# A reciprocal sent through DRAM in place of TensorE broadcasts, and a third Strassen chunk, in a four-layer linear-attention kernel

## The chip, the cores and the metric

The kernel runs on one core of one Trainium2 chip. The metric is device time of that core in microseconds (us), the median of several runs. A run that took over 1.5% longer than the fastest of the same kernel counts as slow and is left out.

## The reference

Two attention layers and two feed-forward layers (FFN) alternate on 2048 tokens of width 512. The attention is linear: no softmax, but a positive feature map, and every query's result is divided by a denominator per head.

```python
def _A_ref(x, wqkv, wo):                       # 32 heads of 16
    qkv = (x @ wqkv)...                        # (cut) split in q, k, v by head
    phi = lambda t: jnp.where(t > 0, t + 1, jnp.exp(t)) + 1e-6
    pq, pk = phi(q), phi(k)
    kv  = jnp.einsum("bhsd,bhse->bhde", pk, v)
    z   = jnp.einsum("bhsd->bhd", pk)
    num = jnp.einsum("bhqd,bhde->bhqe", pq, kv)
    den = jnp.einsum("bhqd,bhd->bhq", pq, z)[..., None] + 1e-6
    return (num / den)... @ wo                 # (cut) heads put back in a row

def _B_ref(x, w1, w2):                         # 512 -> 1376 -> 512
    return jnp.maximum(x @ w1, 0) @ w2

x = A_x
x = x + _A_ref(_layernorm(x), A_wqkv, A_wo)
x = x + _B_ref(_layernorm(x), B_w1, B_w2)
x = x + _A_ref(_layernorm(x), A_wqkv, A_wo)
x = x + _B_ref(_layernorm(x), B_w1, B_w2)
```

## The kernel before

The kernel works in four chunks of 512 tokens per layer. Python code lists all operations once (`g.add` with an engine, what is read, what is written and an estimated duration), and two tables of numbers, `ORDER` and `BANKS`, fix the order in which every engine gets them, the engine of each operation that may run on two (a letter after its number: a for ScalarE, d for VectorE), and the PSUM bank of each result.

The denominators of a chunk come out of four small matmuls that run side by side, each on its own 32 output rows. ScalarE takes a logarithm and an exponential of the negative, which is 1/den for 32 heads. That has to be spread over the 16 features of each head before it can multiply the query features:

```python
def a_den_inv(t, b):
    us = [pq_unit(j, t) for j in range(4)]
    mm_group(lambda: [(psv[32*j:32*j+32, b, :], Zc[:, j, :], unit_ap(us[j]), True, True, False) for j in range(4)], ...)
    ...
    g.add(ACT, lambda e: e.activation(lden[:, s, :], psv[:, b, :], ACTF.Ln, bias=eps6[:, 0:1]), ...)
    g.add(ACT, lambda e: e.activation(lden[:, s, :], lden[:, s, :], ACTF.Exp, scale=-1.0), ...)
    g.add(DVE, lambda e: e.tensor_copy(rhi[:, s, :], lden[:, s, :]), ...)             # bf16 high part
    g.add(DVE, lambda e: e.scalar_tensor_tensor(rsp[:, s, :], rhi[:, s, :], rneg[:, 0:1], lden[:, s, :],
                                                ALU.mult, ALU.add), ...)              # high rows and low rows
    return s

def a_den_mul(t, s, GB):
    us = [pq_unit(j, t) for j in range(4)]
    mm_group(lambda: [(psv[:, GB[j], :], esel[32*j:32*j+32, :], rsp[32*j:32*j+32, s, :], True, True, False)
                      for j in range(4)], ...)                                        # broadcast to 128 rows
    for j in range(4):
        g.add(DVE, lambda e, j=j: e.tensor_tensor(unit_ap(us[j]), unit_ap(us[j]), psv[:, GB[j], :], ALU.mult), ...)
```

In an FFN a chunk's first matmul is done either plainly (`b_h`) or in one level of Strassen (`b_h_str`): seven half-size products in place of eight, for the price of sums of token blocks and of weight blocks on VectorE and of copies between PSUM banks. A parameter names the Strassen chunks of each FFN:

```python
HSTR=[(2, 3), (1, 2, 3)]          # first FFN: chunks 2 and 3; second FFN: chunks 1, 2 and 3
...
hs = HSTR[layer // 2]
for t in range(NCH):
    steps.append((t, None, lambda t=t: b_h_str(t, layer) if t in hs else b_h(t)))
    if t >= 1:
        steps.append((None, None if last_layer else t - 1, lambda t=t: o_step(t - 1)))
```

## Time and profile before

| Kernel before | |
|---|---|
| device time, median of 4 runs | 275.53 us (275.16 to 275.73) |
| span of the profiled run, granted clock | 273.7 us, 0.999 |
| TensorE busy | 267.7 us, 98% |
| VectorE busy | 242.0 us, 88% |
| ScalarE busy | 198.8 us, 73% |
| moved by DMA | 18.35 MB in 41976 packets |

The span is what the profile sees between the first and the last instruction; the device time is some 1.7 us longer. "Busy" adds up the intervals in which an engine had an instruction in flight. It does not say whether an instruction that took longer was waiting for something inside, and of TensorE it says little, because matmuls overlap (one of 512 columns is shown as busy for 379 ns, and the next starts after 216). So the working below takes the distance between starts of consecutive matmuls as their cost. The page, the waits, the stretches and the groups of this kernel are shown in the prediction.

### The profile page before, as it was taken

What the parts mean: (1) busy time and instruction counts of PE and PEld (TensorE: products, weight loads), DVE (VectorE), ACT (ScalarE), POOL (GpSimd) and SP (SyncE); (2) the same over time, 40 slices, a digit from 0 to 9 for tenths busy, and PEclk for the clock granted to TensorE, in tenths of its full rate; (3) what the DMA queues carried; (4) which work ended last, traced back from release to release, by engine and by line L of the source; (5) the groups of instructions that cost most, each with busy time, mean ns of one, the idle gap of its engine ahead of it and who ended that gap; (6) DMA issues with size and microseconds to landing.
All of it is one profiled execution on the core that took longest, in us unless ns stands there. A gap on an engine that the chain in (4) does not pass through costs nothing.

```text
span 273.7 us, 5259 instructions
## 1 busy us (share of the span) xinstructions
PE 267.7 (98%) x1956; PEld 168.0 (61%) x1975; DVE 242.0 (88%) x633; ACT 198.8 (73%) x429; POOL 19.3 (7%) x30
## 2 busy tenths in 40 slices
PE   8999999999999999999999999999999999999995
PEld 3444454444467488888864445355448787888863
DVE  5999799999998998899999837999999899999864
ACT  3988757999974795876679969489998735875320
POOL 3111000000102101000111000000010020110000
PEclk9999999999999999999999999999999999999999
DMA  6955940030462093001226100003310322411012
GB/s 201 383 110 114 294 161 0 13 66 1 77 58 40 6 130 59 4 0 22 39 40 126 27 0 5 0 2 77 60 19 0 79 40 64 111 23 77 2 77 77
DMA packets 41976, 18.35 MB, mean 67 GB/s; under 512 B 36352, under 2 KB 40544, under 8 KB 41952
## 3 DMA queue, kind: packets, MB, share of 16 engines
q1 hardware_dynamic: 41808, 17.96, 28.0%
q8 instruction: 15, 0.25, 0.4%
q14 instruction: 9, 0.07, 0.1%
q10 hardware_dynamic: 144, 0.07, 0.1%
HBM read 7.01 MB, written 2.10 MB: 33 GB/s over the span
## 4 chain that ended last, share of the span: by engine, by line
PE 89%; DVE 5%; ACT 3%; issue 1%
PE ps L535 87%; DVE big L849 2%; PE ps L419 2%; ACT escr L517 2%; ACT big L515 1%; DVE big L521 1%; DVE xn L575 1%; DVE escr L519 0%; ACT big L1016 0%; DVE xn L965 0%; PE ps L498 0%; DVE rsp L839 0%; ACT xn L472 0%; DVE KVT L650 0%; ACT xn L553 0%
## 5 line engine op out<-in xcount | busy, mean ns | idle before, releaser
L517 ACT ACTIVATE escr<-ps 128x512 bf16<-128x512 f32 x60 | 35.4, 611 | 5.8 <-PE ps L535 4.9
L515 ACT ACTIVATE big<-ps 128x512 bf16<-128x512 f32 x60 | 35.5, 612 | 4.3 <-PE ps L535 4.2
L542 ACT ACTIVATE sqscr<-xres 128x512 bf16<-128x512 f32 x48 | 30.1, 627 | 7.3 <-DVE xres L579 3.9
L535 PE MATMUL ps<-big,xn 128*128 128x512 bf16 x123 | 30.2, 379 | 0.3
L535 PE MATMUL ps<-gw,big 128*128 128x512 bf16 x120 | 29.7, 379 | 0.4
L535 PE MATMUL ps<-wqkv,Tb 128*128 128x512 bf16 x124 | 29.7, 379 | 0.4 <-DVE Tb L506 0.2
L1016 ACT ACTIVATE big<-ps 128x512 bf16<-128x512 f32 (+1 forms) x42 | 21.9, 530 | 9.7 <-PE ps L535 9.2
L535 PE MATMUL ps<-Tb,w 128*128 128x512 bf16 x120 | 28.7, 379 | 0.0
L535 PE MATMUL ps<-Tb,wqkv 128*128 128x512 bf16 x112 | 26.6, 379 | 0.0
L521 DVE TENSOR_TENSOR big<-big,escr 128x512 bf16<-128x512 bf16 x60 | 24.2, 421 | 2.4 <-ACT big L515 1.5
L535 PE MATMUL ps<-w,xin 128*128 128x256 bf16 (+1 forms) x190 | 26.1, 272 | 0.0
L519 DVE TENSOR_SCALAR escr<-escr 128x512 bf16<-128x512 bf16 x60 | 16.5, 287 | 7.3 <-ACT escr L517 6.9
L535 PE MATMUL ps<-w2s,big 128*128 128x256 f16 x160 | 21.7, 272 | 0.0
L535 PEld LDWEIGHTS ps<-wqkv,Tb 128*128 128x128 bf16 x128 | 12.3, 98 | 14.7 <-ACT Tb L505 0.7
L535 PEld LDWEIGHTS ps<-big,xn 128*128 128x128 bf16 x128 | 12.0, 98 | 14.6 <-issue 0.9
L849 DVE TENSOR_TENSOR big<-big,ps 128x512 bf16<-128x512 bf16 x32 | 20.5, 680 | 0.5 <-PE ps L535 0.3
L535 PE MATMUL ps<-w,big 128*128 128x256 f16 (+2 forms) x113 | 20.6, 302 | 0.0
L535 PEld LDWEIGHTS ps<-w,xin 128*128 128x128 f16 x190 | 18.3, 98 | 3.7 <-ACT hrt L871 0.2
L568 POOL TENSOR_TENSOR rstdf<-varf,nhalf 128x4 f32<-128x4 f32 x8 | 8.8, 1109 | 161.5 <-DVE varf L566 137.3
L535 PEld LDWEIGHTS ps<-gw,big 128*128 128x128 bf16 x128 | 12.0, 98 | 13.1 <-issue 0.5
L535 PEld LDWEIGHTS ps<-Tb,w 128*128 128x128 bf16 x120 | 11.4, 98 | 12.7 <-issue 0.5
L1099 ACT ACTIVATE ps<-ps 128x256 f32<-128x256 f32 x22 | 8.1, 369 | 15.2 <-PE ps L535 15.0
(154 smaller groups left out, 523.2 us busy)
## 6 DMA issues: line engine op xcount, KB each, us to landing
wqkv<-in_A_wqkv_dram SPq DMA_DIRECT2D x3, 512.0 KB, 7.3
xin<-in_A_x_dram SPq DMA_DIRECT2D x3, 512.0 KB, 8.1
out_dram<-xn SPq DMA_DIRECT2D x3, 512.0 KB, 2.7
w<-in_B_w_dram SPq DMA_DIRECT2D x1, 1376.0 KB, 6.7
w<-in_B_w_dram SPq DMA_DIRECT2D x1, 1280.0 KB, 9.9
wo<-in_A_wo_dram SPq DMA_DIRECT2D x1, 512.0 KB, 10.3
Tb<-xn SPq DMA_TRANSPOSE x30, 3.2
xin<-in_A_x_dram SPq DMA_DIRECT2D x1, 384.0 KB, 3.1
```

Of the source, the lines that this page charges most:

```text
L419: last = e.matmul(psv[:, wt, :], wrm[:, 0:128], wrm[:, :], start=True, stop=True)
L515: g.add(ACT, lambda e: e.activation(dst_ap, psv[:, b, :], ACTF.Identity, bias=1.0 + 1e-6, scale=1.0), [("ps", b)], [dst_key], C_ACT_PSUM, ...
L517: g.add(ACT, lambda e: e.activation(escr[:, s, :], psv[:, b, :], ACTF.Exp), [("ps", b)], [("escr", s)], C_ACT_EXP, name=name + "_exp")
L519: g.add(DVE, lambda e: e.tensor_scalar(escr[:, s, :], escr[:, s, :], 1.0, 1e-6, ALU.min, ALU.add), [("escr", s)], [("escr", s)], C_DVE_BF4 ...
L521: g.add(DVE, lambda e: e.tensor_tensor(dst_ap, dst_ap, escr[:, s, :], ALU.max), [dst_key, ("escr", s)], [dst_key], 340.0, name=name + "_phi")
L535: last = e.matmul(o, l, r, start=st, stop=sp, skip_group_check=skip)
L542: g.add(ACT, lambda e: e.activation(sqscr[:, q, :], xres[:, i, :], ACTF.Square, accum_out=dst[:, i:i + 1]), [("xres", i)], [("sqscr", q), ...
L568: g.add(POOL, lambda e: e.tensor_tensor(rstdf[:, sl], varf[:, sl], nhalf[:, 0:4], ALU.pow), [("varf", t), ("nhalf",)], [("rstdf", t)], C_P ...
L575: g.add(DVE, lambda e: e.scalar_tensor_tensor(xn[:, i, :], psv[:, b, :], rstdf[:, i:i + 1], xres[:, i, :], ALU.mult, ALU.add), rd, [("xn", ...
L849: g.add(DVE, lambda e, j=j: e.tensor_tensor(unit_ap(us[j]), unit_ap(us[j]), psv[:, GB[j], :], ALU.mult), [("big", us[j]), ("ps", GB[j])], ...
L1016: g.add_flex([(ACT, lambda e: e.activation(out_ap(r, m), pv(b), ACTF.Relu), cost(C_ACT_PSUM)), (DVE, lambda e: e.tensor_scalar(out_ap(r, m ...
L1099: g.add_flex([(ACT, lambda e: e.activation(psv[:, c1, cols], psv[:, c2, L], ACTF.Identity), 290.0), (DVE, lambda e: e.tensor_copy(psv[:, c ...
```

## The change

There are two parts, and a new order.

**Part 1.** 1/den is written by the exponential as bf16 straight into `rsp`, stored to DRAM, and read back four times, each read taking 8 rows (8 heads) and repeating each of them 16 times, so that 128 partitions are filled. No TensorE broadcast is left, and no split into high and low parts; the multiplication reads SBUF instead of PSUM. The query projections of the last two chunks of the first attention come late (`QL`).

**Part 2.** The first FFN also gets three Strassen chunks. The weight sums `WN` are kept in one place for both FFNs.

```diff
-HSTR=[(2, 3), (1, 2, 3)]
+HSTR=[(1, 2, 3), (1, 2, 3)]
-QL=(3,)
+QL=(2,)
+        rdram = nc.dram_tensor("rdram", [2, NCH, 128, 512], BF16, kind="Internal").ap()
...
-            g.add(ACT, lambda e: e.activation(lden[:, s, :], lden[:, s, :], ACTF.Exp, scale=-1.0), ...)
-            g.add(DVE, lambda e: e.tensor_copy(rhi[:, s, :], lden[:, s, :]), ...)
-            g.add(DVE, lambda e: e.scalar_tensor_tensor(rsp[:, s, :], rhi[:, s, :], rneg[:, 0:1], lden[:, s, :], ALU.mult, ALU.add), ...)
+            g.add(ACT, lambda e: e.activation(rsp[:, s, :], lden[:, s, :], ACTF.Exp, scale=-1.0), ...)
+            r = rdram[cur_layer[0] // 2, t]
+            dma(lambda e: e.dma_start(r, rsp[:, s, :]), [("rsp", s)], [("rd", t)], 400.0, "rw%d" % t)
+            for j in range(4):
+                i = 4 * t + j
+                dma(lambda e, i=i, j=j: e.dma_start(xn[:, i, :], r[32 * j:32 * j + 8, :].unsqueeze(1).broadcast_to([8, 16, 512])),
+                    [("rd", t)], [("xn", i)], 650.0, "rb%d_%d" % (t, j))
...
-            mm_group(lambda: [(psv[:, GB[j], :], esel[32 * j:32 * j + 32, :], rsp[32 * j:32 * j + 32, s, :], True, True, False)
-                              for j in range(4)], ...)
             for j in range(4):
-                g.add(DVE, lambda e, j=j: e.tensor_tensor(unit_ap(us[j]), unit_ap(us[j]), psv[:, GB[j], :], ALU.mult), ...)
+                i = 4 * t + j
+                g.add(DVE, lambda e, j=j, i=i: e.tensor_tensor(unit_ap(us[j]), unit_ap(us[j]), xn[:, i, :], ALU.mult), ...)
...
-        WN = {1: [... slots(gw_f, "gw", range(3))], 3: [... slots(xin_f, "xin", range(3))]}
+        WN = [(a, [k] + own) for a, k, own in slots(xin_f, "xin", range(3))]
...
-                out[n] = (ap, key)
+                out[n] = (ap, [key] + own)
... (cut: ORDER and BANKS, all numbers new; the places of the row sums, and what else follows from the moved buffers; EARLY, the places of eight sums
     of the second attention; the place of one step of the FFN; the constants for the low parts, which are gone)
```

The last hunk makes the row sums of the second FFN matmul name the buffers under them as well as their own key when they are read. Without it, an order that moves the next writer of such a buffer forward has a race.

## The prediction

> **What bounds the kernel now.** I read the page's busy table first, then its slices, the chain of work that ended last, the waits of TensorE, the stretches of both attention stages, and at last the timeline around the instructions that the change touches.
>
> ```profile
> PE 267.7 (98%) x1956; PEld 168.0 (61%) x1975; DVE 242.0 (88%) x633; ACT 198.8 (73%) x429; POOL 19.3 (7%) x30
> PE   8999999999999999999999999999999999999995
> DVE  5999799999998998899999837999999899999864
> PEclk9999999999999999999999999999999999999999
> PE 89%; DVE 5%; ACT 3%; issue 1%
> ```
>
> The reader sees TensorE busy in every slice at full clock, and 89% of the last chain on it. A busy matmul row need not be a full one, so I looked for idle time and for spacing. The waits of TensorE matmuls hold two entries:
>
> ```profile
> PE ps L419 <- DVE wrm L412: 1.2, 1, 1.2
> PE ps L535 <- DVE Tb L506: 0.2, 1, 0.2
> ```
>
> Both are in the first 9 us. I then took start to start times of consecutive matmuls from the trace: the medians are 216 ns for 512 columns, 109 ns for 256 and 43 ns for 96. After the head (up to 8.6 us) nearly every pair stands at its median. About seventeen gaps are longer by 216 ns almost exactly, which is one 512-column matmul whose record is missing, not idle time. Real slack is about 0.1 us near 180 us and 0.6 us between 262 and 266 us. So what bounds the kernel is **the number of columns TensorE streams**, plus a head of 8.6 us and 3.5 us after the last matmul starts. A change shortens it only by taking TensorE time away, and lengthens it only by opening gaps.
>
> The second engine is close behind, which the stretches show (columns: us, then busy us of PE, PEld, DVE, ACT, POOL with counts):
>
> ```profile
> 38.00:58.00 20.00, 19.87 (x119) 8.77 (x118) 19.19 (x47) 16.16 (x31) 0.00 (x0) 1.00 0.14 27
> 58.00:74.00 16.00, 15.84 (x97) 7.11 (x96) 15.86 (x46) 15.38 (x36) 1.01 (x1) 1.00 0.13 25
> 74.00:110.00 36.00, 35.89 (x277) 25.31 (x278) 32.46 (x88) 25.52 (x58) 4.00 (x4) 1.00 0.43 60
> ```
>
> VectorE is at 96% and 99% in the first attention's end, 90% in the FFN after it.
>
> **What the Trainium skill says, and whether the trace agrees.** (1) "TensorE: Matmul & The Clock Gate", section "Wait — 56ns, not 53.3ns?", gives a warm spacing of N/2.4 GHz plus about 2.5 ns, 215.7 ns for 512 columns; this trace has 216. (2) "TensorEngine Tiling (Array Packing)", section "Key Properties": "Mode switching requires drain". The trace agrees: before each tiled group the spacing is 93 to 96 ns over the median. (3) "VectorE: DVE Perf Modes", section "What auto-detection actually checks": a two-source operation runs two elements per cycle only if every tensor is 16-bit with step one. The trace agrees: 421 ns with bf16 operands alone, 680 ns with the fp32 PSUM operand. (4) "DMA: Bandwidth & Descriptors", section "Anatomy of one DMA — SWDGE (gpsimd) path", fits a fixed cost of about 2.0 us for the GpSimd-issued path. Here the SyncE queue issues; its 128 KB transfers take 1.7 us (store) and 2.4 us (load), so the same order, and I use the trace's figures.
>
> **Part 1, the reciprocal.** For each of 8 chunks (4 in each attention layer) the kernel before turns the denominators into bf16 high and low rows, broadcasts them with four 32-row matmuls, and multiplies from PSUM. This is the timeline of TensorE at one chunk, then the groups concerned:
>
> ```profile
> 170.64 1.24 PE L535 MATMUL ps<-big,xn 128*128 128x512 bf16 x5
> 171.81 0.40 PE L535 MATMUL ps<-rsp,esel 32*128 32x512 bf16 x4
> 172.14 1.04 PE L535 MATMUL ps<-big,xn 128*128 128x512 bf16 x4
> L849 DVE TENSOR_TENSOR big<-big,ps 128x512 bf16<-128x512 bf16 x32 | 20.5, 680 | 0.5 <-PE ps L535 0.3
> L521 DVE TENSOR_TENSOR big<-big,escr 128x512 bf16<-128x512 bf16 x60 | 24.2, 421 | 2.4 <-ACT big L515 1.5
> L839 DVE SCALAR_TENSOR_TENSOR rsp<-rhi,rneg,lden 128x512 bf16<-128x512 bf16 x8 | 6.0, 751 | 0.2
> L838 DVE CAST rhi<-lden 128x512 bf16<-128x512 f32 x8 | 3.4, 421 | 0.2 <-ACT lden L836 0.2
> ```
>
> TensorE, removed: the four matmuls run side by side. The next matmul starts 172.14 - 171.81 = 0.33 us later, and the drain ahead costs 0.095 us: 0.423 us a group. Six groups stand alone, 6 x 0.423 = 2.54 us. Two stand just ahead of the denominator matmuls, which are tiled too and will then pay the drain themselves: one saves 0.33 us, the other, which had a wait of 0.1 us in it, 0.45 us. Sum **3.3 us**, all on the path, since TensorE has no slack.
>
> VectorE, removed: the cast (0.42) and the subtraction (0.75) go. Four multiplications cost 0.62 each back to back now (2.48 us for four in the timeline) and should cost 0.375 each with bf16 operands in SBUF (0.76 us for two of the L521 kind): 0.98 us. Together 2.15 us a chunk, 17 us in all. This lies beside TensorE and buys no time itself.
>
> DMA, added: per chunk one 128 KB write and four 128 KB reads, in 1 KB rows. SyncE issues one in about 0.4 us (the timeline's figure for a 128 KB load). Estimate for one chunk from the end of the exponential: write 1.7, first read issued and landed 0.4 + 2.4, the fourth 1.2 later, last multiplication 0.4: **6.1 us**. The chunk of 167 us takes 4.9 us for the same way now (169.83 to 174.74), another near 62 us 7.1. So the way gets about 1 us longer, and the order of work gives room: it asks for two late query projections instead of one (3.5 us of TensorE work each) and there are FFN matmuls beside. I count 0.
>
> **Part 2, one more Strassen chunk.** The first FFN goes from two to three chunks with seven-product first matmuls. Before: 10 column tiles x 4 matmuls x 216 ns = 8.64 us. After: 7 products x 10 matmuls of 256 columns x 109 ns = 7.63 us. Saved **1.0 us**, on the path. Price beside it: four token sums (4 x 0.42), and for two full groups and a half one an addition, an addition into the output and a rectification (0.69 + 0.69 + 0.29, the half group 1.07): 1.7 + 3.3 + 1.1 = 6.1 us of VectorE. Three PSUM copies a group less one rectification in four cost some 3.5 us more on ScalarE. The W1 block sums are kept over both FFNs, so three sums (3 x 0.82 = 2.5 us of VectorE) go in the second. VectorE: -17 + 6.1 - 2.5, so about 228 us. ScalarE: about 202 us. Neither becomes the bound: from 38 to 142 us VectorE had 97.3 of 104 us; it loses 8.6 and gains 6.1.
>
> **Sum.** 275.4 - 3.3 - 1.0 = 271.1 us. The schedule is a fixed order that was packed for the kernel before without gaps; I allow 0.2 us for a new gap: **271.3 us**, 1.5% faster.
>
> **Rivals.** (a) The bounce through DRAM takes the place of the wait removed: SyncE issues in order, so a read that waits for its write also holds up the transposes behind it (30 of them, 3.2 us to landing), and transfers share engines with them. For it: both waits of the new way are DMA latencies, and 40 issues of 0.4 us are added to one queue. Against it: the DMA share is 0.13 in the stretch of 58 to 74 us, and the change moves its late projections to cover the wait. If each chunk lost 1 us of TensorE, the gain would vanish into 275 us; 0.3 us a chunk gives 273.5. (b) VectorE becomes the bound in the FFN after the first attention, where it is at 90% and takes 6.1 us more in about 36 us, with the chained PSUM copies of Strassen between products. Work can move ahead into the 8.6 us freed before, so I expect at most 1 us: 272. (c) VectorE's relief shortens TensorE's own waits beyond the columns. Against it: there are almost none, 0.7 us after the head. With all of that the time would be 270.4, still within 2%.
>
> **Range and chances.** The column count fixes the gain at 4.3 us, with little spread; rival (c) bounds it below at 270.4, rivals (a) and (b) open it above to 273. Over 2% faster needs under 269.9, more than all the slack that I found: 4%. Slower by over 2% (above 280.9) would need gaps of 10 us: 2%. Within 2%: 94%.
>
> **What would show it right or wrong.** The changed profile should have no 32-row matmuls (32 fewer), matmul spacing still 216 and 109 ns with a sum of gaps under 1 us after the head, VectorE near 228 us, ScalarE near 202, multiplications near 0.4 us, and 40 more DMA issues, with reads landing in 2 to 3 us. Gaps on TensorE released by the multiplications, or by late transposes, would show (a); gaps released by Strassen's copies would show (b). A head or tail changed by over 0.5 us would be outside this reckoning.

## The result, and the profile after

The changed kernel took **271.06 us** (median of 4 runs, 271.01 to 271.46) beside 275.53 us. The ratio is 0.9843, with a 95% interval from 0.9826 to 0.9860. Here and below a ratio is the mean time of one kernel's fast runs over that of the other's in the same rounds, so it is not quite the ratio of the medians quoted. The gain of 4.5 us is 1.6%: inside the predicted range, within 2%.

These are the page's busy line, two of its slices and its last chain, of the kernel after.

```profile
PE 263.8 (98%) x1973; PEld 170.5 (63%) x1973; DVE 232.6 (86%) x635; ACT 196.1 (73%) x426; POOL 18.8 (7%) x30
PE   7999999999999999999999999999999999999995
DVE  4999975999989999999799765599989999979865
PE 92%; DVE 3%; DMA 3%; ACT 1%; issue 0%
```

TensorE is as full as before, in less time, and holds 92% of the last chain. DMA has come into the chain with 3%. VectorE fell from 242.0 to 232.6 us. The waits of TensorE's matmuls (what was waited for, total us, times, longest) are these:

```profile
PE ps L423 <- DVE wrm L416: 1.2, 1, 1.2
PE ps L539 <- DMA Tb<-xn: 0.5, 1, 0.5
PE ps L502 <- DVE xn L1166: 0.3, 1, 0.3
PE ps L539 <- ACT Tb L509: 0.3, 1, 0.3
PE ps L539 <- DVE Tb L510: 0.2, 1, 0.2
```

All but the second are in the head, up to 8.6 us. The second is new: at 157.5 us TensorE waits for a transpose by DMA that makes the input of the second attention. No wait names the trip through DRAM (`xn<-rdram`) or the multiplications. In the matmuls themselves the trace has all 1973 records this time, and none of the 216 ns "gaps" of the kernel before; that they were 19 missing records (1956 of 1975) and not idle time was a reading, which this makes firm.

The stretches of the first attention's end and of the FFN after it, as in the prediction:

```profile
38.00:58.00 20.00, 20.00 (x123) 9.13 (x120) 16.03 (x45) 14.88 (x29) 0.00 (x0) 1.00 0.29 79
58.00:74.00 16.00, 16.00 (x114) 9.54 (x113) 15.28 (x46) 15.73 (x38) 1.07 (x1) 1.00 0.46 107
74.00:110.00 36.00, 36.00 (x303) 27.40 (x302) 33.52 (x93) 26.96 (x63) 3.53 (x3) 1.00 0.38 71
```

VectorE has been relieved where the reciprocal was (19.19 to 16.03 us from 38 to 58 us), and loaded where Strassen was added (32.46 to 33.52 us from 74 to 110). The DMA share rose from 0.14, 0.13 and 0.43 to 0.29, 0.46 and 0.38. Next, the timeline of TensorE at the denominators of two chunks together, near 39 us, and of one chunk, near 168 us (start, us, engine; "x4" joins four):

```profile
39.09 0.61 PE L539 MATMUL ps<-big,Zc 128*32 128x512 bf16 x8
39.64 1.04 PE L539 MATMUL ps<-big,xn 128*128 128x512 bf16 x4
...
167.92 0.40 PE L539 MATMUL ps<-big,Zc 128*32 128x512 bf16 x4
168.25 1.90 PE L539 MATMUL ps<-Tb,wqkv 128*128 128x512 bf16 x8
```

The same on the SyncE queue:

```profile
169.75 0.33 SPq L838 DMA_DIRECT2D rdram<-rsp  x1
171.46 2.49 SPq L841 DMA_DIRECT2D xn<-rdram  x4
```

A group of denominator matmuls holds TensorE for 0.33 us (168.25 - 167.92), plus 0.09 us ahead of it, by which the spacing before a group is longer (the drain). Where two such groups adjoin, at 39.09 us, both together take 0.55 us, not 0.66. For the chunk at 167.92 us the write is issued at 169.75 us, and the reads can be issued only when it has landed, at 171.46. Four issues take 2.49 us, 0.62 each. The groups that answer the prediction's, and then the SyncE queue's own wait:

```profile
L849 DVE TENSOR_TENSOR big<-big,xn 128x512 bf16<-128x512 bf16 x32 | 12.4, 417 | 0.0
L835 ACT ACTIVATE rsp<-lden 128x512 bf16<-128x512 f32 x8 | 5.0, 642 | 0.0
```

```profile
SPq L841 <- DMA rdram<-rsp: 6.4, 5, 1.4
```

The multiplications take 417 ns with both operands as bf16 in SBUF and have no idle time before them: VectorE never stood waiting for a read. The queue stood 6.4 us, in five of eight chunks, waiting for a write, with all that was listed behind it.

**Where the 4.4 us of span went**, from matmul starts. From the first to the last start it is 268.89 us before and 264.89 after, 4.0 less. The broadcasts and denominator groups with their drains cost 3.5 us less, and the matmuls of full height 1.0 us less once the missing records are filled in. Against that, waits over 0.1 us after the head went from 0.5 to 0.8 us, and small delays from 0.6 to 0.8. From the last matmul's start to the end it is 3.55 us before and 3.15 after, 0.4 less.

### The profile page after: what moved, and what is told of

It reads as the page before. It is cut to its first block, busy times and chain, and to the rows that moved or that the text cites. A ratio compares the mean times of both kernels' runs of the same rounds, so it can differ in the third digit from the quotient of the medians.

```text
span 269.3 us, 5317 instructions
## 1 busy us (share of the span) xinstructions
PE 263.8 (98%) x1973; PEld 170.5 (63%) x1973; DVE 232.6 (86%) x635; ACT 196.1 (73%) x426; POOL 18.8 (7%) x30
## 3 DMA queue, kind: packets, MB, share of 16 engines
HBM read 11.21 MB, written 3.15 MB: 53 GB/s over the span
## 4 chain that ended last, share of the span: by engine, by line
PE 92%; DVE 3%; DMA 3%; ACT 1%; issue 0%
PE ps L539 92%; DMA Tb<-xn 2%; DVE bst L446 1%; DMA xin<-in_A_x_dram 1%; DVE xn L478 0%; DVE xn L579 0%; ACT sqscr L546 0%; DVE xn L1166 0%; PE ps L502 0%; DVE mv L447 0%; ACT escr L521 0%; ACT big L519 0%; DVE Tb L510 0%; DVE big L525 0%; DVE xn L1126 0%
## 5 line engine op out<-in xcount | busy, mean ns | idle before, releaser
L521 ACT ACTIVATE escr<-ps 128x512 bf16<-128x512 f32 x60 | 35.7, 606 | 7.8 <-PE ps L539 7.8
L539 PE MATMUL ps<-wqkv,Tb 128*128 128x512 bf16 x128 | 31.2, 379 | 1.0 <-DMA Tb<-xn 0.5
L1015 ACT ACTIVATE big<-ps 128x512 bf16<-128x512 f32 (+1 forms) x47 | 24.9, 536 | 9.6 <-PE ps L539 8.8
L539 PE MATMUL ps<-big,xn 128*128 128x512 bf16 x128 | 30.9, 379 | 0.0
L539 PE MATMUL ps<-w,xin 128*128 128x256 bf16 (+1 forms) x140 | 19.5, 273 | 0.0
L539 PE MATMUL ps<-xn,xin 128*128 128x256 f16 x128 | 19.5, 272 | 0.0
L998 ACT ACTIVATE ps<-ps 128x512 f32<-128x512 f32 (+1 forms) x28 | 14.6, 521 | 5.7 <-PE ps L539 2.8
L539 PEld LDWEIGHTS ps<-Tb,wqkv 128*128 128x128 bf16 x112 | 10.8, 98 | 12.5 <-issue 0.2
L539 PE MATMUL ps<-xn,w 128*128 128x256 f16 x120 | 18.7, 273 | 0.0
L539 PE MATMUL ps<-Tb,w 128*128 128x512 bf16 x80 | 18.4, 379 | 0.0
L539 PE MATMUL ps<-Tb,wper 128*128 128x256 bf16 x120 | 18.3, 273 | 0.0
## 6 DMA issues: line engine op xcount, KB each, us to landing
wo<-in_A_wo_dram SPq DMA_DIRECT2D x1, 512.0 KB, 10.2
```

What stands on the lines that cost most here:

```text
L521: g.add(ACT, lambda e: e.activation(escr[:, s, :], psv[:, b, :], ACTF.Exp), [("ps", b)], [("escr", s)], C_ACT_EXP, name=name + "_exp")
L539: last = e.matmul(o, l, r, start=st, stop=sp, skip_group_check=skip)
L998: g.add_flex([(ACT, lambda e: e.activation(dst(), psv[:, src, 0:W], ACTF.Identity), cost(C_ACT_PSUM)), (DVE, lambda e: e.tensor_copy(dst() ...
L1015: g.add_flex([(ACT, lambda e: e.activation(out_ap(r, m), pv(b), ACTF.Relu), cost(C_ACT_PSUM)), (DVE, lambda e: e.tensor_scalar(out_ap(r, m ...
```

## The experiments

Each ran with a run of the kernel before on the same chip, at 275.3 to 275.9 us in the median. All results were correct. Diffs are against the kernel after, unless said.

### Is it TensorE's columns? One group paid three times

```diff
-            mm_group(lambda: [(psv[32 * j:32 * j + 32, b, :], Zc[:, j, :], unit_ap(us[j]), True, True, False) for j in range(4)],
+            mm_group(lambda: 3 * [(psv[32 * j:32 * j + 32, b, :], Zc[:, j, :], unit_ap(us[j]), True, True, False) for j in range(4)],
```

> The changed kernel with each of the 8 denominator matmul groups issued three times in a row (same result, same order of work otherwise). In the changed trace eight side-by-side denominator matmuls take 0.547 us against 0.332 us for four, so each extra group of four costs 0.215 us of TensorE: 8 x 2 x 0.215 = 3.4 us, about what the removed broadcasts cost (3.3 us). Theory A, the time is the TensorE stream alone: 271.06 + 3.4 = 274.5 us, and the gain shrinks to about 1 us. Theory B, part of the gain came from relief of VectorE or from the waits round the broadcasts: some of the 3.4 us hides beside other waits, and the time is under 273 us.

**Measured:** 274.1 us (274.0 to 274.16), ratio to before 0.9948 (0.9933 to 0.9963): 3.04 us more than the kernel after. The added groups cost 3.45 us by start distances, and the distance from first to last matmul grew by 3.08. The difference is mostly that the wait of 0.6 us for the transpose at 157 us is no longer there, while small new waits add 0.2 to 0.3: a later TensorE meets a transpose that has landed. **What follows:** TensorE time put back, with everything else left as it was, comes back in the device time, but for the wait that it covers. This carries the main step of the prediction.

### Has VectorE room? The multiplications made dearer

```diff
+            def mul(e, j, i):
+                for lo, hi in ((0, 256), (256, 384), (384, 512)):
+                    o = unit_ap(us[j])[:, lo:hi]
+                    last = e.scalar_tensor_tensor(o, o, 1.0, xn[:, i, lo:hi], ALU.mult, ALU.mult)
+                return last
-                g.add(DVE, lambda e, j=j, i=i: e.tensor_tensor(unit_ap(us[j]), unit_ap(us[j]), xn[:, i, :], ALU.mult),
+                g.add(DVE, lambda e, j=j, i=i: mul(e, j, i),
```

> The changed kernel with each of the 32 multiplications split into three slower VectorE instructions (256, 128 and 128 columns, in an operation that takes the one-element rate), correct result. Estimate: 0.43 + 0.29 + 0.29 = 1.0 us in place of 0.42, about 0.58 us each, 18 us of VectorE in all: roughly the relief that the change brought there, put back at the same chunks. Theory A, only TensorE's stream counts and VectorE has room: up to 0.5 us longer, 271.1 to 271.6 us. Theory B, VectorE's relief is what makes the third Strassen chunk and the bounce free: VectorE passes 97% in the stretches of both attention ends and TensorE gets gaps of 2 us or more: over 273 us.

**Measured:** 281.2 us (280.64 to 281.24), ratio 1.0200 (1.0179 to 1.0220): 10.1 us more than the kernel after. VectorE went from 232.6 to 244.4 us, 11.8 more (the estimate of 18 added up durations, which overlap where instructions follow each other), and TensorE's waits over 0.1 us sum up to 12.0. In the waits of TensorE:

```profile
PE ps L539 <- DVE big L850: 3.9, 3, 1.5
PE ps L539 <- DVE varf L570: 1.3, 1, 1.3
```

L850 is the multiplication. **What follows:** nearly all that was added to VectorE came out at the end, so the idea that VectorE at 86% has room for it failed. VectorE was not full, though. Theory B expected over 97% in the stretches of both attention ends; measured are 83% (38 to 58 us), 97% (58 to 74) and 81% (166 to 205). The edit also makes the way of each chunk longer, as the four multiplications come last on it, so load and latency are not told apart by this run alone. The next ones make the trip longer without loading VectorE, and load VectorE away from the trip.

### Has the trip room? One and three more writes

```diff
-            dma(lambda e: e.dma_start(r, rsp[:, s, :]), [("rsp", s)], [("rd", t)], 400.0, "rw%d" % t)
+            op = dma(lambda e: e.dma_start(r, rsp[:, s, :]), [("rsp", s)], [("rd", t)], 400.0, "rw%d" % t)
+            sem = op.seq
+            def again(e):
+                for k in range(1):                     # range(3) in the other run
+                    e.dma_start(r, rsp[:, s, :]).then_inc(sem, 16)
+                    e.wait_ge(sem, 16 * (k + 1))
+                return e.dma_start(r, rsp[:, s, :]).then_inc(sem, 16)
+            op.emit = again                            # those who wait for it wait for 32 (64)
```

The same rows are written to the same place again, one write after the other's landing. No engine but the queue gets work.

> The changed kernel with the 128 KB write of each bounce done twice, the second issued after the first has landed: the way from the exponential to the last multiplication (7.8 to 10.6 us in the changed trace) gets longer by one issue and landing, about 1.75 us, in each of 8 chunks, and the sync queue is held as long. Theory A, the order of work has room for the bounce: at most 0.5 us longer. Rival, the bounce just fits: a gap of up to 1.7 us for each of the chunks without room, 274 us or more.

> As the run with one more write, but three more writes in turn: about 5.2 us longer for each of 8 chunks. It is to find how much room there is: Theory A with a room of about 2 to 3 us a chunk: TensorE waits some 2 to 3 us in several chunks, 278 to 290 us. If the room is over 5 us everywhere: under 272 us. If there is none: 8 x 5.2 = 41 us longer at most, some of it shared where two bounces overlap.

**Measured, one more write:** three fast runs of 276.04, 276.45 and 279.99 us, unusually scattered (a fourth, of 282.25 us, counts as slow), ratio 1.0071 (0.9999 to 1.0144), in the median of the fast ones 5.4 us more than the kernel after. The profiled run is the fastest of them, 276.04 us; from first to last matmul it takes 5.0 us more. The view of the multiplications there, first what VectorE was idle for before them, then who waited for them:

```profile
  DMA xn<-rdram: 5.3, 10
...
  PE ps L540: 2.6, 2
```

In the kernel after, both of these were empty. **Measured, three more writes:** 309.68 us (309.05 to 311.18), ratio 1.1248 (1.1214 to 1.1282), 38.6 us more. Three writes in each of 8 chunks, at 1.7 us, are 41 us. TensorE stands still for 8.7 us near 48 us, 7.5 near 95, and 4.0 near 200 and 241. The expected 278 to 290 us was far too low; "none", 41 us at most, is nearer.

**What follows:** the trip has little room. In the profiled run with one more write some 13.6 us (8 x 1.7) were added and 5.0 came out, so by estimate about 1.1 us a chunk was hidden on average. That fits the slack read from the trace of the kernel after: between a read's landing and the start of its multiplication lie 0.02 to 1.8 us, mostly about 1. Beyond it, latency turns into time almost one for one, with a part of its own for the clock: of the 38.0 us by which the distance from first to last matmul grew with three more writes, some 6 are matmuls of 512 columns that took 0.43 us, at half the granted clock, after the long waits. What is not told apart is the trip itself and what stands behind it: the added writes also hold the SyncE queue with its transposes, and what VectorE has listed behind a multiplication comes late too. Near 48 us, with one more write, VectorE stands idle for 1.7 us until a read lands, makes `KVT` two instructions later, and TensorE waits 1.7 us for `KVT`, which is not on the trip. The prediction's "the order gives room" holds for the trip as it is, and for little more.

### VectorE loaded away from the trip

Half of the row sums of the second FFN matmul (16 of 32) are made by an instruction that takes 1.49 us where the plain one took 0.82. They lie in the FFNs, not on the way of the reciprocal.

```diff
-                g.add_flex([(x, lambda e: e.tensor_tensor(ap, a, b, op), c) for x, c in ((DVE, C_DVE_SUM),)],
+                def row(e):
+                    if n >= 3:
+                        return e.scalar_tensor_tensor(ap, a, 1.0, b, ALU.mult, op)
+                    return e.tensor_tensor(ap, a, b, op)
+                g.add_flex([(x, row, c) for x, c in ((DVE, C_DVE_SUM),)],
```

> The changed kernel with VectorE work added away from the bounce: in each of the 8 FFN chunks two of the four block sums over 128x1280 are done by an operation at the one-element rate, correct result. Estimate: 1280 columns at 512 columns in about 0.68 us less 0.1 fixed make about 1.45 us in place of 0.82, so 0.6 us each, 16 x 0.6 = 10 us of VectorE in all, about as much as the run with the slower multiplications added to VectorE's busy time (11.8 us, which cost 10 us). Theory C, VectorE has little room anywhere, its total is what binds: 277 to 281 us. Theory D, what had no room was the way of the reciprocals, and VectorE in the FFNs has 6 to 14% to spare: within 1 us of the changed kernel, 271 to 272 us.

**Measured:** 278.68 us (278.27 to 278.82), ratio 1.0103 (1.0084 to 1.0122): 7.6 us more than the kernel after, for 16 x 0.67 = 10.7 us of VectorE added. The larger of the changed groups, the stretch of 74 to 110 us, and the two groups of TensorE's waits after the head that are the largest in total:

```profile
L1057 DVE SCALAR_TENSOR_TENSOR xin<-big 128x1280 f16<-128x1280 bf16 x6 | 8.9, 1487 | 0.1
```

```profile
74.00:110.00 36.00, 34.03 (x281) 25.21 (x280) 34.14 (x87) 25.93 (x61) 3.18 (x2) 1.00 0.28 62
```

```profile
PE ps L539 <- DVE ps L1029: 1.7, 3, 0.9
PE ps L539 <- DVE gw L1057: 1.1, 1, 1.1
```

In that stretch VectorE went from 33.52 to 34.14 us of 36, and TensorE fell from 36.00 to 34.03. L1029 is the addition into PSUM inside Strassen, L1057 a dearer row sum itself. **What follows:** VectorE's lack of room is not a matter of the trip alone. Also in the FFNs some 0.7 us are lost for each 1 us added (7.6 of 10.7). It is not that VectorE is full either: it is busy for 88% of this run. The reading that fits is that in a frozen order a VectorE operation that ends later delays the matmuls listed after it. Which of the added time acts by load and which by the longer way to the second FFN matmul, on which the row sums lie, no run tells apart.

### Each part alone: four kernels with an order of their own

A kernel with one part alone has another list of operations, so neither table of order fits it. For all four combinations (neither, part 1, part 2, both) I searched new orders with a list scheduler, which used the durations written in the kernel. Three of the edits:

```diff
 r_part1 (against after):   -HSTR=[(1, 2, 3), (1, 2, 3)]   +HSTR=[(2, 3), (1, 2, 3)]       and new ORDER, BANKS
 r_part2 (against before):  -HSTR=[(2, 3), (1, 2, 3)]      +HSTR=[(1, 2, 3), (1, 2, 3)]    with the moved WN and SUMS, and new ORDER, BANKS
 r_before (against before): -out[n] = (ap, key)            +out[n] = (ap, [key] + own)     and new ORDER, BANKS
```

`r_after` has new tables only. The edit to `r_before` is the one of the change.

> The operations of the kernel before (with a missing read dependency added that the change also adds), in an order and a bank assignment made anew. It is the base for three other runs made by the same search, so that the order is not confounded with the parts. Theory A, TensorE's stream sets the time and the old order had no gaps: 274.5 to 275.5 us, as the kernel before. Rival, the change's gain lies in its new order: a new order of the old operations gets 2 us or more faster, to 273 us or less.

> The changed kernel with only the first part: reciprocals bounced through DRAM, two Strassen chunks in the first FFN, order made anew by the same search. Theory A: the removed broadcasts alone, 3.3 us under r_before, 271.5 to 272.2 us; no gaps on TensorE over 0.5 us. Rival, the DRAM bounce costs gaps that the third Strassen chunk pays for: less than 2 us under r_before.

> The changed kernel with only the second part: three Strassen chunks in each FFN with the new places of the block sums, reciprocals broadcast by TensorE as before; order made anew by the same search. Theory A, TensorE's stream alone: 1.0 us under r_before. Theory B, learnt from the run with VectorE's work put back (281.2 us): the Strassen chunk needs the VectorE time that the first part frees, without it TensorE waits for VectorE: 1 us or more over r_before, with gaps before the output projections and broadcasts of the first attention, and no gain alone.

> All operations of the changed kernel in an order made anew by the same search. Theory A: 1.0 us under r_part1 and 4.3 us under r_before. The changed kernel has one gap of 0.6 us at 157 us; if the new order lacks it, 270.3 to 271.1 us.

**Measured:** 296.18, 287.54, 292.40 and 288.88 us, ratios 1.0738, 1.0414, 1.0617 and 1.0475. All four are far slower than both originals, with waits after the head of 17.5, 10.4, 7.5 and 11.6 us. In three of them the longest is of this kind (here in `r_after`); in `r_part1` it is one of 4.5 us for VectorE (`DVE big L524`). By the clock record TensorE ran at half its clock for 3.4 to 10.2 us of the first 29, most of it during and after these waits:

```profile
PE ps L539 <- DMA wqkv<-in_A_wqkv_dram: 6.8, 1, 6.8
```

The search had moved weight loads to other places; its durations give every transfer a fixed time, whatever else is under way. **What follows:** nothing on the parts. The times expected (270.3 to 275.5 us) were all missed. These runs failed as a test, and they show how far a table fitted to such a model can be off on the chip.

A second set kept the first 31 us of every queue as in the originals, and used longer DMA latencies in the search. The edits are the same but for `ORDER` and `BANKS`; for "neither" the kernel before itself serves.

> Again the first part alone (reciprocals bounced through DRAM, two Strassen chunks in the first FFN), with a new order whose first 31 us on every queue are those of the changed kernel, so that the weight loads stay in their places; in the r_ runs they did not, and TensorE waited 5 to 11 us for them and was throttled afterwards. Theory A: the removed broadcasts alone, 275.4 - 3.3 = 272.1 us, or 271.7 to 272.6. Rival, the bounce costs TensorE gaps that show in the waits: over 273 us.

> Again the second part alone (three Strassen chunks in each FFN, reciprocals broadcast by TensorE as before), with the first 31 us in the order of the kernel before. Theory A, TensorE's stream alone: 275.4 - 1.0 = 274.4 us. Theory B, the extra chunk needs the VectorE time that the first part frees: TensorE gets gaps of 1 us and more in all between 50 and 80 us, behind VectorE, and the kernel is no faster than before: 275.5 to 280 us. The search for an order found none without such gaps, although it found nearly gapless ones for the three other combinations.

> Again both parts in a new order, first 31 us as in the changed kernel. Theory A: 271.1 us less at most the one gap of 0.6 us and 0.3 us at the tail: 270.3 to 271.3 us, and 1.0 us under f_part1.

**Measured**, with the waits after the head and the distance from the first to the last matmul start, from the traces:

| kernel | device us | ratio to before (95%) | first to last matmul | of it waits | rest |
|---|---|---|---|---|---|
| before (original order) | 275.53 | 1 | 268.89 | 0.5 | 268.4 |
| part 1 (`f_part1`) | 276.01 | 1.0025 (0.9991 to 1.0059) | 270.64 | 4.6 | 266.0 |
| part 2 (`f_part2`) | 282.16 | 1.0256 (1.0216 to 1.0296) | 275.87 | 8.7 | 267.1 |
| both (`f_after`) | 277.75 | 1.0091 (1.0065 to 1.0117) | 271.00 | 6.6 | 264.4 |
| after (original order) | 271.06 | 0.9843 (0.9826 to 0.9860) | 264.89 | 0.8 | 264.1 |

All three expected times (272.1, 274.4 and 270.3 to 271.3 us) were missed, and the times do not isolate the parts: the orders' own waits are larger than the parts. `f_after` has the same operations as the kernel after and is 6.7 us slower. In `f_part1` and `f_after`, 1.0 and 0.6 us of TensorE's waits are for the multiplications of part 1 (`DVE big L848`, `L849`), so with other orders the trip, or what stands before it on VectorE, does show. The column "rest", which the waits do not touch, gives -2.4 us for part 1, -1.3 for part 2 and -4.0 to -4.3 for both, to within some tenths. `f_part1` and `f_after` also ran 3.4 us each at half the clock, so their rest is rather too long: by the count of matmuls `f_part1`'s should be 1.0 us above that of the kernel after, and is 1.9; `f_after`'s should equal it, and is 0.3 above. The predicted -3.3, -1.0 and -4.3 fit that. Two stretches of `f_part1` show the clock (the 1.00 and the 0.50):

```profile
38.90:42.30 3.40, 2.46 (x54) 1.84 (x54) 2.59 (x6) 2.74 (x6) 0.00 (x0) 1.00 0.06 16
42.30:45.70 3.40, 3.40 (x14) 0.72 (x13) 3.30 (x9) 1.53 (x3) 0.00 (x0) 0.50 0.00 0
```

The part that did worst is part 2 alone. It has VectorE at 245.6 us (88%), and waits like this one:

```profile
PE ps L539 <- DVE nmf L555: 2.2, 2, 1.4
```

That agrees with the two experiments on VectorE: Strassen's extra work, without the relief by part 1, found no room. It does not prove it, since the search may only have missed a better order.

No run here beats the changed kernel.

## Why the prediction was right

**The bound: right.** TensorE's stream sets the time. Putting TensorE work back brought 3.04 of 3.45 us back, and the trace after has TensorE without a gap after the head but for 0.8 us. Waits over 0.1 us did not fall with the new order (0.5 before), so the gain is not gaps that the order closed.

**Part 1 on TensorE, 3.3 us: right, 3.5 measured.** The excess of 0.2 is at 39.09 us, where two denominator groups adjoin: one drain of 0.09 less, and 0.55 us for both in place of 0.66. Two query projections before them, in place of one, made that possible.

**Part 2 on TensorE, 1.0 us: right.** After minus before, 40 matmuls of 512 columns are gone and 70 of 256 are there; 40 x 0.216 - 70 x 0.109 is 1.0 us, and the spacings are still those.

**The multiplications on VectorE: right.** They take 417 ns, as their model on L521 had it; 8.1 us went there (20.5 to 12.4), where the prediction had 7.8.

**VectorE near 228 and ScalarE near 202: sizes off.** Measured are 232.6 and 196.1 us. The term at fault is the assumption that operations which may run on either engine stay where they were. In the new order plain rectifications of the FFN are 14 on ScalarE and 6 on VectorE, where they were 29 and 1; of the normalisations before the attention, three more are on VectorE. Those moves, with some 1.6 to 3.5 us each, make up most of the 5 us by which VectorE is above, and ScalarE below, the reckoning. The letters in the new `ORDER` said so, and I had not counted them.

**The trip of 6.1 us: too short, 7.8 to 10.6 measured** from the end of the exponential to the end of the last multiplication. The terms: an issue of a broadcast read takes 0.58 us, in the queue's view, not 0.4; a read lands 2.6 to 4.0 us after its issue starts, in the median 3.0, where the 128 KB load showed 2.4 (the sum had 0.4 + 2.4, and so counted the first issue twice); and multiplications are listed about 1 us later than they could start. In three chunks the queue was busy besides: reads were issued 1.3 and 2.2 us after their write had landed, a write 1.7 us after its exponential. The write was right at 1.7 us. That view of the queue's two kinds:

```profile
L841 SPq DMA_DIRECT2D xn<-rdram x32: 577/577/751, 43.1 to 204.0; - x32
L838 SPq DMA_DIRECT2D rdram<-rsp x8: 320/327/360, 41.4 to 200.4; - x8
```

The semaphore records show one way in which a read differs from the 128 KB load that I had taken as its model: that load, like a write, is counted up by 16 landings, a read by one early step and 8 landings. The Trainium skill, "DMA: Bandwidth & Descriptors", section "Why a DMA increments its semaphore by 16 and not by 1", says that the number of engines is the largest up to 16 that divides the slowest dimension of both sides, here 8 rows and 128 partitions, and that the rest of the count is written at once. The trace agrees: 8 landings and one step at about 1.0 us. So each of these reads runs on half of the engines. That this is why it lands later is not shown; no run reads on all 16.

**"I count 0" for the trip: right, but narrowly.** Rival (a) did not come: no wait of TensorE names it. But the two slowed trips show that its room was about 1.1 us a chunk on average. Had the order been packed for the 6.1 us that I reckoned, with no more slack than this one leaves, the real trip should have shown up; no run tried it. The model in the code has a longer trip than I had: 0.47 us for an issue, then 2.5 us to the landing of a write and 2.75 us to that of a read (2.1 us plus the 400 and 650 ns of the diff), with the multiplication some 8 us in all. So the order was made for more than my 6.1.

My reason for the room was a misreading besides. `QL` says how many chunks from the end have their query projections late, so (2,) asks for two in place of three, and not for two in place of one. The traces agree, before and after, with 16 such matmuls to a chunk:

```profile
L535 PE MATMUL ps<-Tb,wqkv x44: 379/379/379, 42.0 to 57.4; 128*128 128x512 bf16 x44
L539 PE MATMUL ps<-Tb,wqkv x32: 379/379/379, 44.8 to 60.7; 128*128 128x512 bf16 x32
```

The change leaves less late projection work beside the trips of the first attention, not more. That the trip cost nothing is thus the work of the order as a whole (the FFN matmuls that I also named are there, from 60.9 us), and as far as the projections go, luck.

**"Neither becomes the bound": true of the result, and the weakest step.** I inferred room from 97.3 busy of 104 us. The runs show that VectorE has next to none in this order, although it is not full: 11.8 us added cost 10.1, 10.7 added cost 7.6. Rival (b), Strassen pressing on VectorE, thus looks like a real danger that part 1's relief, and a new order, kept away; I had treated the relief as something that buys nothing. It buys nothing by itself, but part 2 may need it. Whether part 2 alone could be had without gaps stays open, and so does the exact time of each part alone.

**The allowance of 0.2 us for new waits: 0.5 measured** (0.3 of waits, 0.2 of small delays), with the transpose at 157 us as the largest. The end after the last matmul, 0.4 us shorter, had not been reckoned. These and the 0.2 us of the adjoining groups cancel in part, and the total came out within 0.2 to 0.3 us, closer than its terms.

## What to carry to other kernels

When one engine runs without gaps, count what a change adds to and takes from its stream, from start to start distances; the busy share of a second engine does not tell its room, and a run that makes some of its work dearer does. A latency is hidden only up to its slack, so measure it by adding one hop, and reckon a transfer by one of the same shape, not of the same size. Where an order is frozen, count how it has moved work from one engine to the other, and try any order on the chip before believing the model that made it.

## What the Trainium skill lacked or had wrong

- "DMA: Bandwidth & Descriptors": no issue time by the shape of a transfer. A plain 128 KB write took 0.33 us to issue on the SyncE queue and 1.7 us to land; a read of the same 128 KB, as 8 rows repeated 16 times, took 0.58 us to issue and 2.6 to 4.0 us to land.
- "TensorEngine Tiling (Array Packing)": it says that a change of mode drains, without a size. Here the spacing ahead of a tiled group that stands alone is 92 to 96 ns over the median, and two adjoining denominator groups have that once (they take 0.55 us together, one alone 0.33 us).
- "TensorE: Matmul & The Clock Gate": it describes how idle time lowers the clock, but gives no busy share below which that happens. In `f_part1` the clock fell to half at 42.3 us after 3.4 us in which TensorE was busy for 2.46 us, with no wait over 1.0 us; in the run with one more write it stayed at full from 83.29 to 86.71 us, with TensorE busy for 1.68 us. So the busy share of the profile does not decide it; 48 of the 54 matmuls in the first stretch are of one column, and whether that matters no run tests.
- No page that I read warns that missing matmul records look like idle time: 19 of 1975 were missing before, each a gap of some 216 ns, and none of 1973 after.
